# Later w_down load, finer warming products and short filler writes at the head of a scan-and-GeGLU kernel

## The chip, the core and the metric

The kernel runs on one core of one Trainium2 chip. The core has five engines with an instruction stream each: TensorE (PE: products, with its weight loads listed apart as PEld), VectorE (DVE), ScalarE (ACT), GpSimd (POOL) and SyncE (SP), which here does nothing but issue DMAs. They meet through semaphores. 16 DMA engines move data between the chip's memory (HBM) and the core's (SBUF), and PSUM holds the products. The metric is device microseconds of one execution. Before the change three runs took 179.32, 179.7 and 179.8 us, median 179.7.

## What is computed

The input x has 2048 tokens of 512 features. It is normalized, and goes through two branches that are multiplied at the end:

```python
xn = _layernorm(x, axis=-1)
s = _A_ref(xn, ...)                       # h = Lam_bar * h + Bu[t]; y = 2 Re(h C^T) + xn * Dskip
g = _silu((_gelu(xn @ w_gate) * (xn @ w_up)) @ w_down)
return x + s * g
```

The first branch is a complex diagonal recurrence over the tokens with 512 states; its parameters are dt = exp(log_dt), Lam_bar = exp(dt Lambda), and B scaled by (Lam_bar - 1) / Lambda. The second is a gated feed-forward with 1376 inner features. Types are bf16 with float32 sums.

## The kernel before

The tokens are worked in four slabs of 512, each of four tiles of 128 rows (m = 0 to 3). Nothing in the program loops: about 680 steps, each one a few instructions of one engine, are collected by `Plan.add`, and `Plan.run` emits them in the order of the fixed list `ORDER` (L21). The framework puts in the semaphore waits, from what each instruction reads and writes; the costs and ranks handed to `Plan.add` have no effect on the emitted program any more. So each engine, and SyncE's DMA queue as well, works its steps in the sequence in which they stand in `ORDER`.

The head of the program works on slab 0. The rows of x come in by single tiles (`load_x`, L222) between the four parts of w_up (`load_w`, L213). While x is on its way, TensorE runs products of a constant with itself (`dummies`, L300, seven of 512 columns, then `fill`, L304). VectorE has some `memset`s to do (L225, L250 to L254) and then waits. ScalarE loads its table with one Silu of one column (`tiny`, L257). With x there, `center` subtracts the mean (L341 on ScalarE and L343 on VectorE take half the sum each, L347 subtracts), `head_t` transposes on TensorE (L314, L329) and copies out (L320, L322), and `up_rows` (L402) multiplies by w_up. L615 to L650 work out the parameters and the tables of the recurrence, mostly on VectorE and GpSimd, and `first_w` (L432) makes the remaining up and gate products of slab 0. `first_at` (L445, L447) multiplies gate by up: the gated rows, tile `at`.

The gated rows have to be turned before the product with w_down. `at_t` (L479) does that with a transposing DMA from `at` to `atT`, tile by tile, and `down_pair` (L495) multiplies each tile's 11 blocks by w_down (`wd`), 11 products of 512 columns for a tile. Between the up and gate products of slab 0 and its down products stands `half` (L561), 32 products with the turned B for the recurrence. The scans run on VectorE (L573, L581, L592), and `y_tile` (L511 to L527) brings both branches together.

In the stretch that the change touches, SyncE issues in this order: the turn of xn (L378, two DMAs), B's two turns (L240), w_down's 1280 KB (L695), the turns of the gated rows of tiles 0, 2 and 1 (L479), the turn of slab 1's xn (L378), slab 2 of x (L217), the turn of tile 3's gated rows, and C's two turns (L743). TensorE's order there is the 32 products of L561, then L495 for tiles 0, 2 and 1, then more of L561.

In the listing, `early` is the list of VectorE steps that are to be done before x, and `sb` and `small` allocate SBUF tiles.

Of the kernel before, what the change touches and what calls it, by code (L numbers as in the profile page):

```python
# [10 lines left out]
AF = mybir.ActivationFunctionType  # L11
# [6 lines left out]
PE, ACT, DVE, POOL, SP = "PE", "ACT", "DVE", "POOL", "SP"  # L18


ORDER = (  # L21
# [23 lines left out]
)  # L45


# [33 lines left out]
def kernel(  # L81
# [18 lines left out]
    P = 128  # L100
# [20 lines left out]
    V, A, G, T = nc.vector, nc.scalar, nc.gpsimd, nc.tensor  # L121
    act = A.activation
# [5 lines left out]
    def sb(name, shape, dt=BF16):  # L128
        return consts.tile(shape, dt, name=name)
# [40 lines left out]
    ring = [psum.tile([P, D], FP32, name=f"ring{i}") for i in range(NR)]  # L170
    ybank = [psum.tile([P, D], FP32, name=f"ybank{i}") for i in range(2)]

    def small(name, w=NPT):
        return sb(name, [P, w], FP32)

    pl = Plan()
    DV, AC = 0.075, 0.075

    def dve(n, emit, reads=(), writes=(), rate=1.0, base=DV, **kw):
        return pl.add(DVE, base + n / 960.0 / rate, emit, reads, writes, lag=0.13, **kw)  # L180

    def acts(n, emit, reads=(), writes=(), ptr=0, **kw):
        return pl.add(ACT, AC + 0.12 * ptr + n / 1200.0, emit, reads, writes, lag=0.16, **kw)
# [55 lines left out]
    for ri, src in enumerate((A_B_re, A_B_im)):  # L239
# [9 lines left out]
    warm = nc.const_aps.tensor(1.0, [P, TS], BF16)  # L249
    early = [dve(1, lambda: V.memset(halfpi[:], math.pi / 2), writes=["halfpi"], rank=900.0),  # L250
             dve(4, lambda: V.memset(mhalf[:], -0.5), writes=["mhalf"], rank=900.0),
             dve(4, lambda: V.memset(e_t[:], math.e), writes=["e_t"], rank=900.0)]
    for i in range(NAT):
        early.append(dve(32, lambda i=i: V.memset(at[i][:, F:FP], 0.0), writes=[("atpad", i)], rank=900.0))  # L254
    one = nc.const_aps.tensor(1.0, [P, 1], FP32)

    acts(1, lambda: act(out=tiny[:], in_=one, func=AF.Silu), [], ["tiny"], rank=910.0, not_before=0.72)  # L257
    iota_i = sb("iota_i", [P, NBA], I32)
    iota_f = small("iota_f", NBA)

# [35 lines left out]

    def dummies(k, i):
        def f():
            for j in range(k):
                T.matmul(ybank[j][:] if j < 2 else ring[i][:], lhsT=warm[:, 0:P], rhs=warm, start=True, stop=True)  # L300
        pl.add(PE, k * 0.427, f, [], [("bank", i), ("y", 0), ("y", 1)], lag=0.22, not_before=0.6)

    def fill(w, i):
# [440 lines left out]
    for pt in range(NPT):  # L744
# [3 lines left out]
            out=C2[:, 0, pt, :], in0=CT[:, 0, pt, :], scalar=cre[:, pt : pt + 1], in1=tF[:, 1, :], op0=ALU.mult, op1=ALU.subtract),  # L748
            ["coef", ("CT", 0), ("tF",)], [("C2", 0, pt)], base=0.13)
        dve(512, lambda pt=pt: V.scalar_tensor_tensor(  # L750
            out=C2[:, 1, pt, :], in0=CT[:, 1, pt, :], scalar=ncre[:, pt : pt + 1], in1=tF[:, 0, :], op0=ALU.mult, op1=ALU.subtract),
# [104 lines left out]
```

## Time and profile before

| | us |
|---|---|
| runs | 179.32, 179.7, 179.8 |
| the profiled execution: its time | 179.31 |
| its span, first to last instruction | 177.5 |
| TensorE busy | 172.5 |
| VectorE busy | 157.5 |
| ScalarE busy | 123.9 |
| GpSimd busy | 11.3 |
| first L495 product starts at | 31.95 |

The span begins with the first instruction of the program, and all start times count from there; the 1.8 us between span and time lie around the program. A row of the time line gives start, length, engine, line and operation, output<-inputs, shape and count; in brackets stands how long the engine had been idle and what released it. A row of the chain has start, length and what ran. A row of waits gives total, times and longest. A row by stretches gives, for each engine, busy time and instructions, then the granted clock, the DMA share and GB/s. Lengths of TensorE products include the drain through the array, so that products 0.216 us apart are listed as 0.38 long. "SPq" rows are DMA issues: the length is that of the issue, not of the transfer.

### The profile page before, as it was taken

Reading aid. Unit: us, or ns where it says so; the run is one execution under the profiler, and the core shown is the slowest. Engines: PE = TensorE matmul, PEld = TensorE weight load, DVE = VectorE, ACT = ScalarE, POOL = GpSimd, SP = SyncE. Lnnn points to the kernel's source line nnn. Section 1 sums busy time; section 2 is a strip of 40 time slices with the busy share of each in tenths; the row PEclk is TensorE's granted clock in tenths of the full one; section 3 lists DMA queues with packets and bytes.
Section 4 is the critical chain, followed back from the end, with each engine's and each line's share of the span. In section 5 each row is a group of like instructions: output and inputs, shape, how many; then the busy total and the mean of one; then the engine's idle time right before and its main releaser. Section 6 shows DMA issues by size and latency. Waiting matters only on the chain.

```text
span 177.5 us, 2427 instructions
## 1 busy us (share of the span) xinstructions
PE 172.5 (97%) x846; PEld 82.3 (46%) x846; DVE 157.5 (89%) x256; ACT 123.9 (70%) x238; POOL 11.3 (6%) x26
## 2 busy tenths in 40 slices
PE   8999999899999999999999999999999999999992
PEld 3455453344455544444445454444444455444451
DVE  3678999999699994999979999899999999999754
ACT  6689989839999999899578855373148618572240
POOL 2472030000200000000040000000000000000000
PEclk9999999999999999999999999999999999999999
DMA  5999999999000709414000064094000006626122
GB/s 164 286 344 229 177 264 227 214 265 212 0 0 0 197 3 185 99 61 80 0 0 6 24 135 101 30 192 85 0 0 0 0 30 144 83 52 140 37 62 77
DMA packets 48355, 18.66 MB, mean 105 GB/s; under 512 B 40312, under 2 KB 47832, under 8 KB 48344
## 3 DMA queue, kind: packets, MB, share of 16 engines
q1 hardware_dynamic: 48344, 18.52, 47.7%
q8 instruction: 6, 0.10, 0.2%
q14 instruction: 5, 0.04, 0.1%
HBM read 6.46 MB, written 2.10 MB: 48 GB/s over the span
## 4 chain that ended last, share of the span: by engine, by line
PE 84%; DVE 7%; DMA 5%; POOL 2%; issue 0%; DVEq 0%
PE ring L463 31%; PE ring L495 22%; PE ybank L511 15%; PE ring L561 12%; DMA atT<-at 5%; PE ring L402 2%; DVE st L281 2%; DVE Q L650 1%; PE ring L300 1%; DVE yg L516 1%; DVE tab L650 1%; POOL dt__137 L618 1%; PE ybank L300 1%; DVE junk L522 1%; POOL rho L622 1%; POOL rs L293 0%
## 5 line engine op out<-in xcount | busy, mean ns | idle before, releaser
L463 PEld LDWEIGHTS <-xnT 128*128 128x128 bf16 x288 | 28.2, 98 | 28.4
L495 PE MATMUL ring<-wd,atT 128*128 128x512 bf16 (+1 forms) x176 | 39.4, 379 | 1.1 <-DMA atT<-at 1.1
L463 PE MATMUL ring<-wg,xnT 128*128 128x512 bf16 (+1 forms) x144 | 31.6, 357 | 0.0
L463 PE MATMUL ring<-wu,xnT 128*128 128x512 bf16 (+1 forms) x144 | 31.3, 357 | 0.0
L561 PE MATMUL ring<-xnT,BT 128*128 128x512 bf16 x128 | 30.1, 379 | 0.0
L592 DVE TENSOR_TENSOR_SCAN Fs<-rho,ini,W 128x512 bf16<-128x512 f32 x24 | 29.7, 1272 | 0.1
L466 ACT ACTIVATE ub<-ring 128x512 bf16<-128x512 f32 (+1 forms) x36 | 19.2, 555 | 13.7 <-PE ring L463 13.5
L511 PE MATMUL ybank<-C,hst 128*128 128x512 bf16 x120 | 27.7, 379 | 0.0
L495 PEld LDWEIGHTS <-atT 128*128 128x128 bf16 (+1 forms) x176 | 17.1, 98 | 22.1 <-DMA atT<-at 1.5
L563 ACT ACTIVATE U<-ring 128x512 bf16<-128x512 f32 x32 | 18.1, 599 | 7.3 <-PE ring L561 7.3
L466 ACT ACTIVATE gt<-ring 128x512 bf16<-128x512 f32 (+1 forms) x36 | 19.5, 556 | 3.7 <-PE ring L463 3.5
L498 ACT ACTIVATE g<-ring 128x512 f32<-128x512 f32 x16 | 9.4, 594 | 15.5 <-PE ring L495 15.3
L511 PEld LDWEIGHTS <-hst 128*128 128x128 bf16 x136 | 13.3, 98 | 14.0
L561 PEld LDWEIGHTS <-BT 128*128 128x128 bf16 x128 | 12.5, 98 | 14.8
L573 DVE TENSOR_TENSOR Q<-U,tab 128x4096 bf16<-128x4096 bf16 x8 | 18.3, 2289 | 0.9 <-ACT tab L657 0.7
L573 DVE TENSOR_TENSOR Q<-Fs,tab 128x4096 bf16<-128x4096 bf16 x8 | 18.3, 2288 | 0.1
L516 DVE TENSOR_TENSOR yg<-ybank,g 128x512 bf16<-128x512 f32 x15 | 10.2, 685 | 5.8 <-PE ybank L511 5.7
L774 ACT ACTIVATE junk<-x_tok 128x512 bf16<-128x512 bf16 x16 | 10.0, 632 | 1.3 <-DMA x_tok<-in_A_x_dram 1.3
L507 ACT ACTIVATE ybank<-sk 128x512 f32<-128x512 bf16 x15 | 9.1, 604 | 1.7 <-DVE yg L516 1.6
L779 ACT ACTIVATE xna<-x_tok,nb,rs 128x512 bf16<-128x512 bf16 x12 | 9.5, 812 | 0.0
L592 DVE TENSOR_TENSOR_SCAN Fs<-rho,W 128x512 bf16<-128x512 f32 x8 | 9.3, 1211 | 0.1
L472 DVE TENSOR_TENSOR at<-gt,ub 128x1024 bf16<-128x1024 bf16 x12 | 8.2, 684 | 0.0
(149 smaller groups left out, 172.0 us busy)
## 6 DMA issues: line engine op xcount, KB each, us to landing
x_tok<-in_A_x_dram SPq DMA_DIRECT2D x3, 512.0 KB, 4.2
out_dram<-ot SPq DMA_DIRECT2D x12, 128.0 KB, 2.1
wd<-in_B_w_down_dram SPq DMA_DIRECT2D x1, 1280.0 KB, 7.9
wu<-in_B_w_up_dram SPq DMA_DIRECT2D x4, 256.0 KB, 3.5
wg<-in_B_w_gate_dram SPq DMA_DIRECT2D x1, 864.0 KB, 8.0
x_tok<-in_A_x_dram SPq DMA_DIRECT2D x4, 128.0 KB, 4.2
wg<-in_B_w_gate_dram SPq DMA_DIRECT2D x1, 512.0 KB, 5.9
wu<-in_B_w_up_dram SPq DMA_DIRECT2D x1, 352.0 KB, 5.0
```

What stands on the lines that cost most here:

```text
L463: T.matmul(ps[:, 0 : b - a], lhsT=xnT[:, s % 2, m, k, :], rhs=wt[:, k, a:b], start=(k == 0), stop=(k == KT - 1))
L466: acts(b - a, lambda: act(out=dst[:, a:b], in_=ps[:, 0 : b - a], func=AF.Copy if up else AF.Gelu_apprx_tanh), [("bank", r)], [key], table= ...
L495: T.matmul(ps[:], lhsT=atT[:fs, k, m * P : (m + 1) * P], rhs=wd[:fs, k, :], start=(k == 0), stop=(k == NFT - 1))
L498: acts(512, lambda b=b, ps=ps: act(out=g2[gi][:, b, :], in_=ps[:], func=AF.Silu), [("bank", r)], [("g2", gi, b)], table="silu", rank=3.0)
L511: T.matmul(ps, lhsT=hst[s % 2][:, j // NPT, j % NPT, m * P : (m + 1) * P], rhs=C2[:, j // NPT, j % NPT, c0:c1], start=(j == 0 and not seed ...
L516: dve(w, lambda: V.tensor_tensor(out=yg[e][:, c0:c1], in0=ps, in1=g2[gi][:, b, c0:c1], op=ALU.mult), [key, ("g2", gi, b)], [("yg", e, c0)])
L561: T.matmul(ps[:], lhsT=BT[:, ri, k, pt * P : (pt + 1) * P], rhs=xnT[:, s % 2, :, k, :], start=(k == 0), stop=(k == KT - 1))
L563: acts(512, lambda q=q, ri=ri, ps=ps: act(out=U[ui][:, ri, q, :], in_=ps[:], func=AF.Copy), [("bank", r)], [("U", ui, q, ri)])
L573: dve(4096, lambda: V.tensor_tensor(out=Qf, in0=src.unsqueeze(1).to_broadcast(WQ), in1=table, op=ALU.mult), reads, ["Q"], rate=2.0)
L592: pl.add(DVE, 1.12 if s == 0 else 1.185, lambda ri=ri, q=q, pt=pt, first=first: V.tensor_tensor_scan(out=Fs[:, ri, q, :], data0=rho[:, pt ...
L774: acts(512, lambda i=i, fn=fn, sc=sc, m=m: act(out=junk()[:], in_=x_tok[:, s * M + m, :], func=fn, scale=sc, accum_out=sx[:, s, i, m : m + ...
L779: acts(512, lambda m=m: act(out=xn[m], in_=x_tok[:, s * M + m, :], func=AF.Identity, scale=rs[:, s, m : m + 1], bias=nb[:, s, m : m + 1]), ...
```

## The change

Four things change, all of them in what is issued in the first 25 us.

1. w_down's load (its step is 121 in the old list and 123 in the new one) stands behind the turn of tile 0's gated rows, step 162 in the new numbering, and ahead of tile 2's. Before, it stood right behind B's turns (steps 15 and 16).
2. `dummies` issues 28 products of 128 columns where it issued 7 of 512. They write the first 128 columns of the same banks: the first two the y banks, all others one ring bank.
3. A new step `pads` writes one column of a new tile `pad` 30 times on VectorE, last of what VectorE does before x.
4. A new step makes three Silus of one column into a new tile `tail2` on ScalarE, behind `tiny`.

All other numbers of `ORDER` are the old ones, renumbered for the two new steps (21 is `pads`, 27 the Silus); nothing else is moved. In the diff, the list is cut to the lines with these steps.

```diff
 ORDER = (
-    25, 26, 1, 29, 27, 24, 22, 23, 21, 2, 3, 4, 5, 6, 38, 19, 20, 17, 18, 0, 30, 31, 32, 39, 7, 8, 9, 10, 11, 28, 33, 35, 34, 36, 37, 54, 55, 57, 58,
...
-    15, 164, 168, 183, 165, 169, 228, 233, 16, 121, 166, 170, 185, 187, 167, 189, 231, 171, 230, 229, 184, 186, 362, 190, 188, 172, 173, 174, 176,
-    175, 177, 178, 179, 180, 181, 182, 191, 160, 237, 238, 162, 241, 242, 161, 239, 232, 245, 247, 262, 279, 287, 284, 283, 280, 286, 248, 263, 240,
...
+    26, 27, 28, 1, 31, 29, 25, 23, 24, 22, 2, 3, 4, 5, 6, 40, 19, 20, 17, 18, 0, 21, 32, 33, 34, 41, 7, 8, 9, 10, 11, 30, 35, 37, 36, 38, 39, 56, 57,
...
+    160, 161, 147, 15, 166, 170, 185, 167, 171, 230, 235, 16, 168, 172, 187, 189, 169, 191, 233, 173, 232, 231, 186, 188, 364, 192, 190, 174, 175,
+    176, 178, 177, 179, 180, 181, 182, 183, 184, 193, 162, 123, 239, 240, 164, 243, 244, 163, 241, 234, 247, 249, 264, 281, 289, 286, 285, 282, 288,
...
@@ -250,11 +250,19 @@
              dve(4, lambda: V.memset(e_t[:], math.e), writes=["e_t"], rank=900.0)]
+    pad = small("pad", 1)
+
+    def pads():
+        for _ in range(30):
+            V.memset(pad[:], 0.0)
+    early.append(pl.add(DVE, 0.90, pads, [], ["pad"], rank=900.0, not_before=0.72))
     for i in range(NAT):
...
     acts(1, lambda: act(out=tiny[:], in_=one, func=AF.Silu), [], ["tiny"], rank=910.0, not_before=0.72)
+    tail2 = small("tail2", 1)
+    acts(1, lambda: [act(out=tail2[:], in_=one, func=AF.Silu) for _ in range(3)], [], ["tail2"], rank=880.0)
...
     def dummies(k, i):
         def f():
-            for j in range(k):
-                T.matmul(ybank[j][:] if j < 2 else ring[i][:], lhsT=warm[:, 0:P], rhs=warm, start=True, stop=True)
+            for j in range(4 * k):
+                T.matmul((ybank[j][:] if j < 2 else ring[i][:])[:, 0:P], lhsT=warm[:, 0:P], rhs=warm[:, 0:P], start=True, stop=True)
         pl.add(PE, k * 0.427, f, [], [("bank", i), ("y", 0), ("y", 1)], lag=0.22, not_before=0.6)
```

40 rows, old and new, of the table ORDER are left out of this document.

## The prediction

> **What bounds the kernel now.** I read the page first (busy shares and the chain that ended last), then the waits of TensorE, then the time line around its one wait, and from there the queue that it waited for.
>
> ```profile
> PE 172.5 (97%) x846; PEld 82.3 (46%) x846; DVE 157.5 (89%) x256; ACT 123.9 (70%) x238; POOL 11.3 (6%) x26
> PE 84%; DVE 7%; DMA 5%; POOL 2%; issue 0%; DVEq 0%
> PE ring L495 <- DMA atT<-at: 1.1, 1, 1.1
> PE ybank L300 <- PEq L840: 0.8, 1, 0.8
> 23.83 7.07 PE L561 MATMUL ring<-xnT,BT 128*128 128x512 bf16 x32
> 31.95 0.39 PE L495 MATMUL ring<-wd,atT 128*128 128x512 bf16 x1 [1.06 <-DMA atT<-at]
> ```
>
> TensorE is busy 97% of the span, 84% of the last chain is its products, and behind the start of the program it waits once. The 32 products of L561 start 0.216 us apart ((7.07 - 0.38) / 31), so the last slot ends at 23.83 + 32 x 0.216 = 30.74; L495 opens at 31.95. That hole of 1.2 us is all that a better order can win. It also cuts the other way: whatever delays TensorE before 30.74 costs nothing until it has used up the 1.2 us.
>
> What the hole waits for is the chain in its stretch and the SyncE queue:
>
> ```profile
> 20.62 0.60 DVE at L445
> 21.13 0.34 DVE L447 TENSOR_TENSOR at<-gt,at 128x352 bf16<-128x352 bf16 x1
> 22.66 9.24 DMA atT<-at
> 19.89 2.04 SPq L240 DMA_TRANSPOSE BT<-in_A_B_im_dram  x1
> 21.98 0.58 SPq L695 DMA_DIRECT2D wd<-in_B_w_down_dram  x1
> 22.66 5.57 SPq L479 DMA_TRANSPOSE atT<-at  x1
> BT<-in_A_B_im_dram SPq DMA_TRANSPOSE x1, 4.5
> wd<-in_B_w_down_dram SPq DMA_DIRECT2D x1, 1280.0 KB, 7.9
> atT<-at SPq DMA_TRANSPOSE x16, 3.7
> L479 SPq DMA_TRANSPOSE atT<-at x16: 1262/1396/5568, 22.7 to 159.8; - x16
> ```
>
> (Start and length; for the queue rows the last number is the median time to landing.) The first gated rows are ready at 21.13 + 0.34 = 21.47, their turn is issued at 22.66 behind w_down's 1280 KB, and it takes 9.24 us where the median is 3.7: landed at 31.9. w_down itself lands at 21.98 + 7.9 = 29.9, the B turn before it at 19.89 + 4.5 = 24.4, so w_down has the queue for 5.5 us. L495 needs both.
>
> **The change, part by part.** *w_down behind the first turn.* On SyncE the 0.58 us issue is moved past one turn's issue (1.4 us by the median; the 5.57 came from standing behind w_down). The first turn no longer waits for w_down, and lands about 3.7 us after its issue. w_down starts when that turn is through, 5.5 us of queue as before. With nothing else changed: issue at 22.0, rows landed at 25.7, but not before B is out (24.4) plus a turn; w_down at 25.7 + 5.5 = 31.2 instead of 29.9. So the hole's end goes from 31.95 (rows) to about 31.2 (w_down): -0.7 us. Bounds: w_down moving as soon as it is issued, 23.4 + 5.5 = 28.9, so that the hole closes fully (-1.2); or its whole 7.9 us behind the end of its own issue, 24.0 + 7.9 = 31.9 (no gain). I take the middle one, since it is how w_down stood to the turn ahead of it in this trace. Queued behind it on SyncE: the second turn lands 2.0 us behind w_down (31.9 against 29.9 for the turn that stands there now), and L495's second group needs it 11 x 0.216 = 2.4 us after the first opens: covered by 0.4 us. The later items (third turn, next xnT, slab 2) have the same work ahead of them as before.
>
> *28 products of 128 columns for 7 of 512, and the head of the program.*
>
> ```profile
> 0.76 1.01 PE L300 MATMUL ybank<-const-bfloat16-1.0 128*128 128x512 bf16 x2 [0.76 <-PEq L840]
> 3.70 0.42 PE L304 MATMUL ring<-const-bfloat16-1.0 128*128 128x256 bf16 x1
> 3.80 0.47 PEld L314 LDWEIGHTS <-xna 128*128 128x128 bf16 x4 [0.38 <-DVE xna L347]
> 4.12 0.43 PE ring L314 x4
> 4.57 0.41 PE L329 MATMUL ybank<-ident,xna 128*128 128x128 bf16 x4
> 4.75 0.22 PE ybank L329 x4
> 4.98 3.04 PE ring L402 x14
> ```
>
> Four 128-column products with their weight loads take 0.43 us here (L314 in the chain), 0.107 each; 28 are 3.0 us against 3.70 - 0.76 = 2.94 now: +0.05. If the weight load sets the pace (0.47 / 4) it is 3.3 us, +0.35. Either way they end before x is ready on the rows below, so nothing lands on the path. By the same rows the array doubles its pace between L314 (0.107 each) and L329 (0.22 / 4 = 0.055), some 3.8 us after the first product.
>
> *30 one-column writes on VectorE.*
>
> ```profile
> 0.80 0.16 DVE L254 MEMSET at<- 128x16 uint32 x4 [0.80 <-PEq L840]
> L250 DVE MEMSET halfpi<- 128x1 f32 x1 | 0.1, 59 | 0.0
> 1.00 0.11 DVE L225 MEMSET pv<- 128x64 uint32 x1
> 2.79 0.49 DVE L343 TENSOR_SCALAR_CACHE_REDUCE yg<-x_tok 128x320 bf16<-128x320 bf16 x1 [1.67 <-DMA x_tok<-in_A_x_dram]
> 3.40 0.60 DVE L347 TENSOR_SCALAR xna<-x_tok,ma,mb 128x256 bf16<-128x256 bf16 x2
> 4.43 0.28 DVE L320 COPY W<-ring 128x256 bf16<-128x256 bf16 x1
> 45.91 0.16 DVE L788 SCALAR_TENSOR_TENSOR sx<-sx,mq 128x4 f32<-128x4 f32 x1
> 46.11 0.17 DVE L789 TENSOR_SCALAR sx<-sx 128x4 f32<-128x4 f32 x1
> ```
>
> VectorE idles 1.67 us before x. Writes to different tiles run 0.03 us apart (four in 0.16, each 0.07 long): 30 would take 0.9 us, hidden. But all 30 write the same tile. Where one VectorE instruction touches what the one before it wrote, the next starts 0.04 us after the first has ended (45.91 + 0.16 to 46.11). At 0.059 + 0.04, say 0.095 each, 30 take 2.85 us: from 1.04 to 3.9, and L343 starts 1.1 us later than 2.79. These are the two ends, 0 and 1.1 us. I take the long one: the writes share a tile, as L788 and L789 do and the four fast ones do not. Who waits: L347 (3.40 to 4.5), its transposes on TensorE (ready at 3.80, run from 3.91 behind the fill, so 1.0 late: 4.9), L320 behind them (about 0.9 late), and so the products of L402: d = 0.9 us on TensorE, with real gaps between 4.0 and 5.8.
>
> *Three more one-column Silus on ScalarE*, between the first one and x:
>
> ```profile
> 2.01 0.20 ACT L257 ACTIVATE tiny<-const-float32-1.0 128x1 f32<-128x1 f32 x1
> 2.79 0.36 ACT L341 ACTIVATE junk<-x_tok 128x192 bf16<-128x192 bf16 x1 [0.57 <-DMA x_tok<-in_A_x_dram]
> ```
>
> At 0.2 to 0.25 us each they end between 2.8 and 2.95; at worst 0.15 us late, under VectorE's 1.1. Without that cover: 0.15 us on the head.
>
> *Longer programs.* The change adds 42 instructions to TensorE, 30 to VectorE, 3 to ScalarE, and the program itself is fetched by the same DMA engines:
>
> ```profile
> q8 instruction: 1, 0.02, 16.1%
> 18.70:20.20 1.50, 1.50 (x10) 0.78 (x8) 1.47 (x4) 1.50 (x4) 0.00 (x0) 1.00 1.36 37
> 20.20:21.70 1.50, 1.50 (x9) 0.69 (x7) 1.50 (x4) 1.50 (x4) 0.00 (x0) 1.00 1.21 270
> ```
>
> A 16 KB block comes in between 17.9 and 18.4 (the first row is the DMA view of that stretch), and right behind it the B turn falls to 37 GB/s for 1.5 us, from about 270. TensorE passes 2 x 846 instructions in 177.5 us, 9.5 per us, so 42 more bring its block 4.4 us earlier, to about 14 us + d, amid plain loads. If the block is what stalls the turn, the B turns are out up to 1.3 us sooner. In the sum this is worth nothing, because the gated rows, not B, then start the first turn; it counts in a rival below. The bounds: -1.3 to +1.3 us on the queue (the stall may hit the xnT turns there).
>
> *The sum.* TensorE reaches L495 at 30.74 + 0.9 = 31.64. The gated rows, whose inputs come through TensorE and the parameter chain, are ready at 21.47 + 0.9 = 22.37, landed 26.07, w_down at 31.57. L495 opens at 31.65, 0.3 us earlier than now. Then the rest must follow:
>
> ```profile
> 47.83 0.75 DVE L750 SCALAR_TENSOR_TENSOR C<-hst,ncre,tF 128x512 bf16<-128x512 bf16 x1 [1.54 <-ACT tF L745]
> 64.23 0.69 DVE L581 TENSOR_TENSOR hst<-Q 128x1024 bf16<-128x1024 bf16 x1
> 65.51 0.59 PE L511 MATMUL ybank<-C,hst 128*128 128x512 bf16 x2
> ```
>
> VectorE, 0.9 us late, has a hole of 1.54 us before 47.83; the first L511 has 0.6 us between its last input (64.92) and its start. Both cover the shift, so the 0.3 us is kept to the end: 179.31 - 0.3 = 179.0 for the profiled execution, which is 0.4 under the median of the runs (179.7). Against the median: **179.4**.
>
> **The rivals.**
>
> *B, the writes are cheap* (0.03 us each, d = 0). Rows ready at 21.47, TensorE at 30.74. If the block is what stalls B, B is out at 23.1, the first turn lands at 21.5 + 3.7 = 25.2, w_down at 30.7: the hole is gone, -1.2, 178.5. For: the fast memsets, and the TensorE products that rewrite one bank without waiting. Against: L788/L789. The Trainium skill ("Runtime: NRT & Kernel Launch", Instruction fetch mechanics) calls the cost of crossing a 16 KiB block mostly hidden; by that B would still be out at 24.4 and w_down land at 31.2, -0.7 and 179.0. The 37 GB/s row speaks against the page.
>
> *C, slower: the array stays at half pace.* Now the products run without a gap from 0.76 to the doubling at about 4.57. With x 1.1 us late they stop at about 4.0. If the stretch must be unbroken and starts again at 4.9, full pace comes at 4.9 + 3.8 = 8.7, and the products from 5.8 to 8.7 run at half pace: 1.45 us lost, d = 2.35, beyond the hole by 1.15 us: 180.8. It decides once d exceeds 1.2. For: the doubling behind 3.8 dense us. Against: the gap starts when most of that stretch is over. The Trainium skill ("TensorE: Matmul & The Clock Gate", The HAM clock gate) has the pace released after one busy window of about 3.4 us that runs freely; by that, 4.0 - 0.76 = 3.2 us is just short, and the loss would be as worked out here. The trace agrees with the length, and shows no interrupted case.
>
> *D, slower: w_down takes the place of the rows.* Its 7.9 us behind its issue at 23.8 give 31.7 to 32.3, and a fetched block (1.3 us) in w_down or in the second turn puts L495 or its second group 0.9 us late: 180.6. For: nothing is faster in total on that queue, two transfers have only changed places. Against: 0.4 us of cover. Without the block it is no change, 179.7.
>
> **How the numbers follow.** A measurement of this kernel tells about 0.3% (0.54 us) from no change. Chances: my forecast 0.40 (178.9 to 179.9 by the bounds of its terms), B 0.22, C 0.20, D 0.18. Faster: a quarter of mine and most of B, 0.30. Slower: C, most of D and a tenth of mine, 0.39. The same: 0.31. The range reaches from B (178.5) to C (180.8).
>
> **What would show it.** In the new trace: the spacing of the 30 writes (0.03 or 0.095) and the start of L343 (2.8 or 3.9); the pace of L402 (0.216 or 0.43); the first turn's landing within about 4 us of its issue; L495's wait, now put down to w_down or gone; the stretch behind 18 us at 270 GB/s and the block's fetch near 15. The prediction is wrong if L343 starts on time, if L402 runs at half pace, or if a new wait of TensorE stands later in the chain.

## The result and the profile after

The changed kernel takes 181.41 us (median of 22 runs, 179.82 to 182.46) against 179.72 us before (22 runs): ratio 1.0085, 95% interval 1.0063 to 1.0106. It is slower by 1.7 us, where 179.4 us and a range of 178.5 to 180.8 us were predicted. The ratios, here and below, leave out a kernel's slow runs (three of ten at most), while the medians take in all of its runs. The profiled execution took 181.15 us with a span of 179.3 us, 1.84 us and 1.8 us more than before.

Lines of the page after, with the chain that ended last, and below it the waits of TensorE (total, times, longest):

```profile
PE 172.9 (96%) x851; PEld 84.8 (47%) x867; DVE 158.9 (89%) x286; ACT 124.3 (69%) x241; POOL 11.2 (6%) x26
...
PE 94%; DVE 3%; issue 2%; DVEq 0%
...
wd<-in_B_w_down_dram SPq DMA_DIRECT2D x1, 1280.0 KB, 7.6
```

```profile
PE ring L322 <- DVE xna L355: 1.6, 1, 1.6
```

The 1.1 us wait at the first down product is gone, as intended. DMA has left the chain altogether (5% before). In its place stands a new wait of 1.6 us, for the centred x, at the head of the program. The head and the early stages in the time line after (start, length, engine, line; everything behind the new writes stands 8 lines lower: L351 is the old L343, L410 the old L402, L569 the old L561, L503 the old L495, L455 the old L447, L487 the old L479, L703 the old L695):

```profile
1.07 3.58 DVE L257 MEMSET pad<- 128x1 f32 x29
4.69 0.48 DVE L351 TENSOR_SCALAR_CACHE_REDUCE yg<-x_tok 128x320 bf16<-128x320 bf16 x1
...
24.11 0.33 DVE L455 TENSOR_TENSOR at<-gt,at 128x352 bf16<-128x352 bf16 x1
...
3.70 0.42 PE L312 MATMUL ring<-const-bfloat16-1.0 128*128 128x256 bf16 x1
5.71 0.65 PE L322 MATMUL ring<-ident,xna 128*128 128x128 bf16 x4 [1.59 <-DVE xna L355]
...
6.79 2.48 PE L410 MATMUL ring<-wu,W 128*128 128x512 bf16 x6
...
10.83 0.39 PE L337 MATMUL ring<-ident,xna 128*128 128x128 bf16 x4
...
26.81 7.07 PE L569 MATMUL ring<-xnT,BT 128*128 128x512 bf16 x32
33.71 2.54 PE L503 MATMUL ring<-wd,atT 128*128 128x512 bf16 x10
...
19.27 2.15 SPq L240 DMA_TRANSPOSE BT<-in_A_B_re_dram  x1
...
24.47 1.38 SPq L487 DMA_TRANSPOSE atT<-at  x1
25.90 0.78 SPq L703 DMA_DIRECT2D wd<-in_B_w_down_dram  x1
```

Three things are to be read here. The first 29 of the 30 writes take 3.58 us, so one starts (3.58 - 0.06) / 28 = 0.126 us after another, and VectorE takes up x at 4.69 instead of 2.79: 1.90 us late. TensorE stands still from the end of its filler to 5.71. And then the first six of the up products (L410; the view ends at 9 us, and so does this row) run (2.48 - 0.38) / 5 = 0.42 us apart, half the array's pace; from the first of them to the transposes behind the fourteenth it takes 10.83 - 6.79 = 4.04 us, where 14 products at full pace are 3.03 us. The trace's record of the granted clock says the same: it begins, with full clock, at 8.84 us, where the kernel before has full clock from 4.62 us.

The delay adds up along TensorE. x's first transpose starts at 5.71 instead of 3.91 (1.80), the transposes themselves take 1.08 us instead of 0.90 (0.18), and the up products lose 4.04 - 3.03 = 1.01. That is 2.99 us, and the 32 products of L569 are through at 26.81 + 6.91 = 33.72 instead of 30.74: 2.98. The old hole of 1.21 us absorbs its share, and the first down product starts at 33.71 instead of 31.95, 1.76 us later. The span is 1.8 us longer, so nothing behind that point takes from or adds to the difference.

The first turn works as foreseen: issued at 24.47, when its rows are there (24.11 + 0.33), and no longer behind w_down. w_down lands at 25.90 + 7.6 = 33.5, just ahead of TensorE.

### The profile page after: what moved, and what is told of

Its sections match the earlier page's. It is cut to its first block, busy times and chain, and to the rows that moved or that the text cites. A ratio compares the mean times of both kernels' runs of the same rounds, so it can differ in the third digit from the quotient of the medians.

```text
span 179.3 us, 2485 instructions
## 1 busy us (share of the span) xinstructions
PE 172.9 (96%) x851; PEld 84.8 (47%) x867; DVE 158.9 (89%) x286; ACT 124.3 (69%) x241; POOL 11.2 (6%) x26
## 4 chain that ended last, share of the span: by engine, by line
PE 94%; DVE 3%; issue 2%; DVEq 0%
PE ring L471 31%; PE ring L503 21%; PE ring L569 15%; PE ybank L519 14%; PE ring L440 5%; PE ring L410 4%; PE ybank L440 2%; DVE pad L257 1%; DVE yg L524 1%; DVE junk L530 1%; PE ring L322 0%; PE ybank L337 0%; DVE xna L355 0%; PE ring L337 0%; PE ring L312 0%
## 5 line engine op out<-in xcount | busy, mean ns | idle before, releaser
L503 PE MATMUL ring<-wd,atT 128*128 128x512 bf16 (+1 forms) x170 | 38.9, 379 | 0.3
L569 PE MATMUL ring<-xnT,BT 128*128 128x512 bf16 x128 | 30.1, 379 | 0.0
L503 PEld LDWEIGHTS <-atT 128*128 128x128 bf16 (+1 forms) x176 | 17.1, 98 | 20.9 <-DMA atT<-at 0.3
L569 PEld LDWEIGHTS <-BT 128*128 128x128 bf16 x128 | 12.5, 98 | 14.7
L581 DVE TENSOR_TENSOR Q<-U,tab 128x4096 bf16<-128x4096 bf16 x8 | 18.3, 2289 | 0.9 <-ACT tab L665 0.7
L581 DVE TENSOR_TENSOR Q<-Fs,tab 128x4096 bf16<-128x4096 bf16 x8 | 18.3, 2287 | 0.1
(151 smaller groups left out, 177.9 us busy)
```

Of the source, the lines that this page charges most:

```text
L503: T.matmul(ps[:], lhsT=atT[:fs, k, m * P : (m + 1) * P], rhs=wd[:fs, k, :], start=(k == 0), stop=(k == NFT - 1))
L569: T.matmul(ps[:], lhsT=BT[:, ri, k, pt * P : (pt + 1) * P], rhs=xnT[:, s % 2, :, k, :], start=(k == 0), stop=(k == KT - 1))
L581: dve(4096, lambda: V.tensor_tensor(out=Qf, in0=src.unsqueeze(1).to_broadcast(WQ), in1=table, op=ALU.mult), reads, ["Q"], rate=2.0)
```

## The experiments

All of them are small edits of the changed kernel or of the kernel before. The table holds what decides: when VectorE takes up x, when TensorE is through with the 32 products (start of their row + 32 x 0.216), when w_down has landed (its issue plus its time to landing, by the trace), when the first down product starts, and the span. The ratio is to runs of the kernel before on the same chip.

| kernel | x | 32 products | w_down | first down product | span | median | ratio [95%] |
|---|---|---|---|---|---|---|---|
| before | 2.79 | 30.74 | 29.9 | 31.95 | 177.5 | 179.7 | 1 |
| changed | 4.69 | 33.72 | 33.5 | 33.71 | 179.3 | 181.41 | 1.0085 [1.0063, 1.0106] |
| without the writes | 2.77 | 31.20 | 30.3 | 31.19 | 176.8 | 179.04 | 0.9966 [0.9941, 0.9992] |
| a tile for each write | 2.78 | 30.99 | 31.4 | 31.40 | 177.4 | 179.16 | 0.9942 [0.9909, 0.9975] |
| moved load alone | 2.77 | 31.23 | 32.0 | 32.07 | 177.9 | 179.23 | 0.9954 [0.9928, 0.9981] |
| writes alone | 4.69 | 33.71 | 32.2 | 34.25 | 179.8 | 181.99 | 1.0114 [1.0089, 1.0139] |
| 52 warming products | 4.69 | 32.39 | 31.6 | 32.38 | 177.9 | 180.0 | 1.0025 [0.9996, 1.0055] |
| 14 writes | 2.87 | 31.28 | 30.3 | 31.27 | 176.8 | 179.1 | 0.9960 [0.9933, 0.9987] |
| 28 products alone | 2.77 | 31.01 | 30.2 | 32.29 | 177.8 | 179.67 | 0.9998 [0.9970, 1.0027] |
| load and products | 2.75 | 30.94 | 30.2 | 30.93 | 176.5 | 179.15 | 0.9965 [0.9937, 0.9993] |
| 22 writes | 3.70 | 31.66 | 32.0 | 32.09 | 177.8 | 180.02 | 1.0014 [0.9987, 1.0042] |
| 38 warming products | 4.70 | 32.40 | 32.7 | 32.70 | 178.9 | 179.98 | 1.0014 [0.9993, 1.0035] |
| coarse products, late x | 4.70 | 33.66 | 34.3 | 34.30 | 180.0 | 181.99 | 1.0089 [1.0044, 1.0134] |

In every row the span is the start of the first down product plus 145.5 to 146.2 us. To within 0.7 us, the changes of this case are decided by that one moment.

**Without the writes.**

```diff
     def pads():
-        for _ in range(30):
-            V.memset(pad[:], 0.0)
+        pass
```

> The changed kernel without its 30 one-column writes; the moved load, the 28 products and the three Silus stay. Theory (the writes are the loss: x 1.9 us late on VectorE, and about 1 us more while the array goes on at half pace): L343's counterpart starts near 2.8 again, the up products run 0.216 us apart from the first, the 32 products before the first down product end near 30.75, and what is left of the hole is w_down, landing between 30.4 and 31.2. Time 178.2 to 179.0, 0.4 to 0.8% under the kernel before. Rival (the moved load or the shifted program costs the time, the writes only hide it): w_down lands at 32 or later and the time stays at 180 or above.

Its time line (lines stand one higher than in the changed kernel: L350 is its L351), and the loading of w_down on its page:

```profile
2.77 0.49 DVE L350 TENSOR_SCALAR_CACHE_REDUCE yg<-x_tok 128x320 bf16<-128x320 bf16 x1 [1.65 <-DMA x_tok<-in_A_x_dram]
...
4.72 3.30 PE L409 MATMUL ring<-wu,W 128*128 128x512 bf16 x14
...
31.19 5.14 PE L502 MATMUL ring<-wd,atT 128*128 128x512 bf16 x23
...
23.84 0.60 SPq L702 DMA_DIRECT2D wd<-in_B_w_down_dram  x1
```

```profile
wd<-in_B_w_down_dram SPq DMA_DIRECT2D x1, 1280.0 KB, 6.5
```

179.04 us, ratio 0.9966, just above what was expected (at most 179.0): without the writes the rest of the change is a gain. x is on time, the up products run at full pace, w_down is there at 30.3, and TensorE goes into the down products without waiting. The rival, that the moved load itself costs the time, has fallen.

**A tile for each write.**

```diff
-    pad = small("pad", 1)
+    pad = [small(f"pad{i}", 1) for i in range(30)]
...
-        for _ in range(30):
-            V.memset(pad[:], 0.0)
+        for i in range(30):
+            V.memset(pad[i][:], 0.0)
```

> The changed kernel, but each of the 30 one-column writes goes to a tile of its own: as many instructions, no two on the same tile. Theory (a write that waits for the one before it costs 0.125 us, one that does not 0.03 us): the writes take about 0.9 us and end near 2.0, x is taken up at 2.8 as before, and the time is that of the kernel without the writes, 178.2 to 179.0. Rival (any 30 writes cost 0.125 us each): 181.2 to 181.6 as in the changed kernel. Second rival (the longer program moves its own loading into the way): writes short and x on time, but time at 180 or above.

```profile
1.07 0.83 DVE L257 MEMSET pad<- 128x1 f32 x30
2.78 0.48 DVE L351 TENSOR_SCALAR_CACHE_REDUCE yg<-x_tok 128x320 bf16<-128x320 bf16 x1 [0.88 <-DMA x_tok<-in_A_x_dram]
```

The same 30 instructions now take 0.83 us instead of 3.7: one starts (0.83 - 0.06) / 29 = 0.027 us after another. VectorE is done 0.88 us before x arrives, and the time is 179.16 us. Neither the number of writes nor the longer program costs anything; the order among writes to one tile, which the framework keeps with a wait, costs 0.1 us each.

**The moved load alone** (the kernel before, with one number moved):

```diff
-    15, 164, 168, 183, 165, 169, 228, 233, 16, 121, 166, 170, 185, 187, 167, 189, 231, 171, 230, 229, 184, 186, 362, 190, 188, 172, 173, 174, 176,
-    175, 177, 178, 179, 180, 181, 182, 191, 160, 237, 238, 162, 241, 242, 161, 239, 232, 245, 247, 262, 279, 287, 284, 283, 280, 286, 248, 263, 240,
+    15, 164, 168, 183, 165, 169, 228, 233, 16, 166, 170, 185, 187, 167, 189, 231, 171, 230, 229, 184, 186, 362, 190, 188, 172, 173, 174, 176,
+    175, 177, 178, 179, 180, 181, 182, 191, 160, 121, 237, 238, 162, 241, 242, 161, 239, 232, 245, 247, 262, 279, 287, 284, 283, 280, 286, 248, 263, 240,
```

> The kernel before with the moved load alone. Theory as in the prediction: the first turn lands about 4 us after its issue, w_down at 31.2 (bounds 30.0 and 31.9), L495 opens 0.7 us earlier: 179.0. Rival: w_down lands no earlier than the rows did (31.9 or later), 179.7 to 180.6.

```profile
4.98 3.53 PE L402 MATMUL ring<-wu,W 128*128 128x512 bf16 x14
...
32.07 4.27 PE L495 MATMUL ring<-wd,atT 128*128 128x512 bf16 x19 [0.68 <-DMA wd<-in_B_w_down_dram]
...
16.99 4.21 SPq L240 DMA_TRANSPOSE BT<-in_A_B_re_dram  x1
...
23.38 1.55 SPq L479 DMA_TRANSPOSE atT<-at  x1
```

179.23 us, ratio 0.9954: faster by 0.5%, as forecast. The one profiled execution (179.71 us) doesn't show it: w_down lands at 32.0, where the rival had it, and the first down product starts at 32.07. Two things came late in it. The pace doubled only among the up products (14 of them take 3.53 us, 3.19 at full pace); that moment differs between profiles (last section). And the issue of the first B turn took 4.21 us; that goes with the seven coarse products (the longer program, below). What the load's move gives is seen better where both are on time (load and products, below).

**The writes alone** (the kernel before, with the 30 writes):

```diff
+    pad = small("pad", 1)
+
+    def pads():
+        for _ in range(30):
+            V.memset(pad[:], 0.0)
+    early.append(pl.add(DVE, 0.90, pads, [], ["pad"], rank=900.0, not_before=0.72))
```

> The kernel before with the 30 writes alone (w_down in its old place, seven products of 512 columns, one Silu). Theory: TensorE comes to the first down product near 33.9 as in the changed kernel, and the rows' turn, behind w_down and with its rows 3 us later, lands near 34: 181.6 to 182.2. Rival (the finer products are what leaves the array at half pace): only the 1.9 us of x arrive there, less the 1.2 us of the hole: 180.4 to 180.8.

```profile
6.79 2.47 PE L410 MATMUL ring<-wu,W 128*128 128x512 bf16 x6
...
26.80 7.07 PE L569 MATMUL ring<-xnT,BT 128*128 128x512 bf16 x32
34.25 2.12 PE L503 MATMUL ring<-wd,atT 128*128 128x512 bf16 x9 [0.38 <-DMA atT<-at]
...
25.89 8.97 SPq L487 DMA_TRANSPOSE atT<-at  x3
```

181.99 us, ratio 1.0114. TensorE is through at 33.71, as in the changed kernel, at half pace in the same place, without the finer products. The rows' turn, behind w_down, lands at 34.2 and leaves a hole of its own. The writes alone account for the whole loss.

**52 warming products**, which bridge the gap.

```diff
-            for j in range(4 * k):
+            for j in range(4 * k + 24):
```

> The changed kernel with 24 more warming products (52 instead of 28), so that TensorE works on until x, late by the 30 writes, is there at 5.7. Theory (the 1.6 us gap sends the array back to the start of its warming, which costs about 1 us of half pace behind it): pace doubles near 4.5 and stays, the up products start at 0.216 us, TensorE comes to the first down product near 32.8 instead of 33.9, w_down lands about 1 us earlier as well, time 180.2 to 180.7. Rival (the pace does not depend on the gap, or w_down at 33.5 is the bound by itself): 181.2 to 181.6 as in the changed kernel.

```profile
0.93 4.82 PE L308 MATMUL ring<-const-bfloat16-1.0 128*128 128x128 bf16 x50
...
5.71 0.54 PE L322 MATMUL ring<-ident,xna 128*128 128x128 bf16 x4
...
6.46 2.77 PE L410 MATMUL ring<-wu,W 128*128 128x512 bf16 x11
...
32.38 3.84 PE L503 MATMUL ring<-wd,atT 128*128 128x512 bf16 x16
```

180.0 us, ratio 1.0025 [0.9996, 1.0055], clear of the changed kernel's 1.0085 [1.0063, 1.0106]. That is 0.2 us below what was expected. x is as late as there, its first transpose starts at the same 5.71, and nothing else was edited. But the array works until then and goes over to its full pace on the way (at 4.74; 50 products take 4.82 us, and 0.107 us each would be 5.3), and TensorE reaches the first down product at 32.38 instead of 33.71. So the gap costs 1.33 us (0.33 in the transposes, which take 0.75 instead of 1.08 us, and 1.0 in the up products, 3.04 us from the first to the transposes behind the fourteenth instead of 4.04), besides what the late x costs by itself.

**14 writes.**

```diff
-        for _ in range(30):
+        for _ in range(14):
```

> The changed kernel with 14 writes to the one tile instead of 30. Theory (they cost 0.125 us each, and only what reaches past x's arrival at 2.8 counts): they end at 1.07 + 14 x 0.125 = 2.82, x is taken up at 2.8 to 2.85, the rest is as without writes: 179.0 to 179.3. Rival (each write costs something wherever it stands): about half way, 180.2.

```profile
1.07 1.70 DVE L257 MEMSET pad<- 128x1 f32 x14
2.87 0.49 DVE L351 TENSOR_SCALAR_CACHE_REDUCE yg<-x_tok 128x320 bf16<-128x320 bf16 x1
```

179.1 us, ratio 0.9960. (1.70 - 0.06) / 13 = 0.126 us each again; they fit before x, and cost nothing.

**28 products alone** (the kernel before, with the new `dummies`).

```diff
-            for j in range(k):
-                T.matmul(ybank[j][:] if j < 2 else ring[i][:], lhsT=warm[:, 0:P], rhs=warm, start=True, stop=True)
+            for j in range(4 * k):
+                T.matmul((ybank[j][:] if j < 2 else ring[i][:])[:, 0:P], lhsT=warm[:, 0:P], rhs=warm[:, 0:P], start=True, stop=True)
```

> The kernel before with the 28 products of 128 columns for the seven of 512, nothing else. Theory as in the prediction (they end at the same time, and the block of program that comes in 4 us earlier is worth nothing in the sum, because w_down still stands ahead of the first turn): first turn landed at 31.7 to 32.0, 179.5 to 180.0. Rival (the earlier block clears the queue in front of B's turns, 1 us or more for everything behind): first turn landed at 30.8 or earlier, 178.8 to 179.2.

```profile
17.16 2.21 SPq L240 DMA_TRANSPOSE BT<-in_A_B_re_dram  x1
...
22.53 10.05 SPq L486 DMA_TRANSPOSE atT<-at  x3
...
32.29 4.06 PE L502 MATMUL ring<-wd,atT 128*128 128x512 bf16 x17 [1.11 <-DMA atT<-at]
```

179.67 us, ratio 0.9998. The issue of the first B turn isn't held up here (2.21 us), but that of the second takes 2.40, so that both are over at 21.81, as good as before (21.94), and the rows' turn, behind w_down, lands at 32.2. The prediction gave this term nothing, and within the 0.3% of the interval that is what it is worth.

**Load and products** (the changed kernel without the writes and without the three Silus).

```diff
     def pads():
-        for _ in range(30):
-            V.memset(pad[:], 0.0)
+        pass
...
-    acts(1, lambda: [act(out=tail2[:], in_=one, func=AF.Silu) for _ in range(3)], [], ["tail2"], rank=880.0)
+    acts(1, lambda: [], [], ["tail2"], rank=880.0)
```

> The kernel before with the moved load and the 28 products, without the writes and the three Silus. Theory: as without the writes alone, 178.8 to 179.2, w_down landing near 30.4, before or just when TensorE gets there; the Silus are worth nothing. Rival (the Silus cost or bring 0.1 to 0.2 us by way of ScalarE's half of the sum): 0.15 us away from that, which shows in the start of the first VectorE copy, not in the time.

```profile
3.63 0.27 PE L311 MATMUL ring<-const-bfloat16-1.0 128*128 128x256 bf16 x1
...
30.93 5.35 PE L502 MATMUL ring<-wd,atT 128*128 128x512 bf16 x23
...
21.06 0.34 DVE L454 TENSOR_TENSOR at<-gt,at 128x352 bf16<-128x352 bf16 x1
...
17.18 2.27 SPq L240 DMA_TRANSPOSE BT<-in_A_B_re_dram  x1
19.49 2.05 SPq L240 DMA_TRANSPOSE BT<-in_A_B_im_dram  x1
21.64 1.50 SPq L486 DMA_TRANSPOSE atT<-at  x1
23.18 0.91 SPq L702 DMA_DIRECT2D wd<-in_B_w_down_dram  x1
```

179.15 us, ratio 0.9965 [0.9937, 0.9993]. The Silus are worth nothing that these runs show (179.04 with them). w_down lands at 30.2, and the hole is closed: the first down product at 30.93, 1.02 us earlier than before. Against the products alone the move brings 0.5 us by the medians. This kernel, like the other four with x on time and the load moved, is faster than both the kernel before and the changed one.

**22 writes.**

```diff
-        for _ in range(30):
+        for _ in range(22):
```

> The changed kernel with 22 writes to the one tile instead of 30: x is taken up at 1.07 + 22 x 0.125 = 3.8, 1.0 us late as the prediction had it, and TensorE's gap before x's transposes is 0.6 to 0.7 us instead of 1.6. Theory A (any gap before the pace has doubled starts its stretch again): full pace comes 3 us after x's first transpose, near 7.7, about 1 us is lost, TensorE comes to the first down product near 32.7, and the time is 180.1 to 180.6. Theory B, the prediction's own case (the stretch goes on across a gap so short): full pace before 5.8, first down product at 31.6 to 31.8, time 179.0 to 179.5.

```profile
4.71 0.65 PE L322 MATMUL ring<-ident,xna 128*128 128x128 bf16 x4 [0.59 <-DVE xna L355]
...
5.75 3.19 PE L410 MATMUL ring<-wu,W 128*128 128x512 bf16 x14
...
32.09 6.21 PE L503 MATMUL ring<-wd,atT 128*128 128x512 bf16 x28 [0.26 <-DMA wd<-in_B_w_down_dram]
...
19.95 2.90 SPq L240 DMA_TRANSPOSE BT<-in_A_B_im_dram  x1
22.95 1.60 SPq L487 DMA_TRANSPOSE atT<-at  x1
```

This is close to the prediction's own case: x is taken up 0.9 us late, where the prediction had 1.1. Theory B has the pace right: with a gap of 0.59 us all 14 up products run 0.216 us apart, and TensorE is through at 31.66 (31.64 was predicted; that the two agree so closely is luck, since x is 0.2 us less late and the transposes, in part at half pace, take 1.04 us instead of 0.90). The time is between the two expectations, 180.02 us, because w_down came at 32.0 and not at 31.57.

**38 warming products** (30 writes).

```diff
-            for j in range(4 * k):
+            for j in range(4 * k + 10):
```

> The changed kernel with 10 more warming products (38): they run past the doubling, as the 24 more did, but stop near 4.8, so that a gap of about 0.9 us stands between the doubling and x's transposes at 5.7. Theory A (a gap costs only when it falls into the stretch before the doubling; a pace once granted outlives 0.9 us): the up products start 0.216 us apart, time as with 24 more, 179.8 to 180.4. Theory B (any gap takes the pace back): the up products start 0.43 us apart until 8.5 or later, time 181.1 to 181.6.

```profile
4.76 0.42 PE L312 MATMUL ring<-const-bfloat16-1.0 128*128 128x256 bf16 x1
5.70 0.55 PE L322 MATMUL ring<-ident,xna 128*128 128x128 bf16 x4 [0.52 <-DVE xna L355]
...
6.49 2.76 PE L410 MATMUL ring<-wu,W 128*128 128x512 bf16 x12
```

179.98 us, ratio 1.0014: Theory A's time, but the run doesn't test what it was made for. The filler at 4.76 is still at half pace (0.42 us long; 0.27 at full pace), so the doubling came behind the gap, not ahead of it. It is a second case of a gap of half a microsecond that didn't hold the doubling back. No run here puts a gap of 0.9 us behind the doubling.

**The changed kernel with the load in its old place.**

```diff
-    176, 178, 177, 179, 180, 181, 182, 183, 184, 193, 162, 123, 239, 240, 164, 243, 244, 163, 241, 234, 247, 249, 264, 281, 289, 286, 285, 282, 288,
+    176, 178, 177, 179, 180, 181, 182, 183, 184, 193, 162, 239, 240, 164, 243, 244, 163, 241, 234, 247, 249, 264, 281, 289, 286, 285, 282, 288,
```

(and 123 behind 16 in the line above it.)

> The changed kernel with w_down's load in its old place; the 30 writes, the 28 products and the Silus stay. The move: by the comparison with and without it when x is on time (0.3 to 0.5%), the time is 0.3 to 0.5% above the changed kernel, 181.9 to 182.3; rival, with TensorE at 33.7 the move has nothing left to win, 181.4. The pace: this run has the same 1.6 us gap. If the stretch starts again with the product behind the gap, the pace doubles at 8.8 once more; if the chip watches fixed stretches of time that do not follow the kernel, the doubling falls elsewhere, before the gap or between 7 and 9.1.

181.64 us, ratio 1.0059 [1.0020, 1.0098]. The interval holds the changed kernel's 1.0085 and, nearly, the 1.0114 of the writes alone. Inconclusive: whether the move is worth anything when x is late is not shown.

```profile
6.79 4.41 PE L410 MATMUL ring<-wu,W 128*128 128x512 bf16 x14
```

Its one profiled execution took 183.18 us, 1.5 us above the median, and is no measure of the move. But it has the gap of 1.6 us too, and full clock only from 9.25 us on, 3.5 us behind x's first transpose: neither at 8.8 nor in the stretch that was named for the other case.

**The changed kernel with the seven coarse products.**

```diff
-            for j in range(4 * k):
-                T.matmul((ybank[j][:] if j < 2 else ring[i][:])[:, 0:P], lhsT=warm[:, 0:P], rhs=warm[:, 0:P], start=True, stop=True)
+            for j in range(k):
+                T.matmul(ybank[j][:] if j < 2 else ring[i][:], lhsT=warm[:, 0:P], rhs=warm, start=True, stop=True)
```

> The changed kernel with the seven products of 512 columns instead of the 28 of 128; the moved load, the 30 writes and the Silus stay. The 28 products are worth nothing: 181.2 to 181.6, as the changed kernel; rival, the finer products set the array back, 180.4 or less. The pace: the same gap of 1.6 us once more; doubling at 8.8 again speaks for a stretch that starts with the product behind the gap, any other moment for fixed stretches of time.

```profile
6.79 4.15 PE L410 MATMUL ring<-wu,W 128*128 128x512 bf16 x14
```

181.99 us, ratio 1.0089, that of the changed kernel (the median is 0.4 us above what was expected): within the half percent of its interval, the finer products neither help nor hurt. The 14 up products take 4.15 us, 0.96 more than the 3.19 at full pace. The clock record has full clock from 8.74 us on here, and from 8.84 in the changed kernel and 8.83 with the writes alone, each time with a gap of 1.6 us and 3.0 to 3.1 us behind x's first transpose.

The single runs say that this loss isn't paid every time. Of the 48 executions of the four kernels with the 1.6 us gap (the changed one, the writes alone, and these last two), eight have spans of 177.9 to 178.7 us, like those of the kernel whose gap is bridged (177.9 to 179.4), and all others 178.9 or more. None of the eight was profiled.

## Why the prediction was wrong

**The failed term: the price of the 30 writes.** The prediction saw that the writes share a tile and must wait for one another, and took the long end of its two bounds: 0.059 + 0.04 us, "say 0.095 each", x 1.1 us late. They cost 0.126 us each, and x was 1.90 us late. The gap of 0.04 us was read between two instructions of 0.16 us; behind one of 0.06 us it is 0.066. Only the bound was wrong, not the reason: with a tile for each write, the same 30 writes cost 0.027 us each and nothing on the path. The Trainium skill ("VectorE: DVE Perf Modes", The DRAIN you can't avoid) reports of eight copies that a semaphore behind each costs nothing extra, and says that a next instruction that isn't held starts earlier. The traces agree with the second: without the wait the writes overlap (0.027 us apart, each 0.06 long), with it they don't. So for writes this small, other than for the eight copies, the wait has a price.

**The failed step: the array's pace.** The forecast had d = 0.9 us on TensorE and no loss of pace in its sum; half pace was its rival C, with a chance of 0.20, and C's outcome is what came. The first down product started at 33.71, where 31.65 was forecast. Of these 2.06 us, 0.75 are the price of the writes (at full pace x's lateness brings TensorE 1.65 us late, as the 52 warming products show, instead of 0.9), and 1.33 the lost pace. C had worked the loss out as 1.45 us, near the 1.33; its 180.8 us is too low because it goes with x 1.1 us late. Its reason, a stretch that must be unbroken and starts again behind the gap, is not what the traces show: a gap of 0.59 us (22 writes) did not put the doubling off, and the last section has what decides. The 52 warming products show that it is the gap and not the late x: with x as late, 1.33 us come back. With a gap of 0.59 us the forecast's way of counting d was sound; its own gap of 0.9 us was not tried.

**w_down.** The move does what it says: moved load alone 0.9954, load and products with the hole closed at 30.93. But for its own case the prediction had w_down at 31.57, and with 22 writes it came at 32.0. The sentence that fails there is that "the gated rows, not B, then start the first turn". (In the changed kernel it holds, since x is later still: B's second turn was issued by 23.88, the rows were ready at 24.44, and the turn went out at 24.47.) With 22 writes the rows were ready on time, at 22.39 (22.37 predicted), but the issue of the second B turn ended at 19.95 + 2.90 = 22.85, and the turn was issued at 22.95. With load and products it is the same: rows at 21.40, B's issue over at 21.54, turn at 21.64. SyncE's own issues, not the rows, start the first turn there. That is 0.5 us, and by the 22 writes it would have made the predicted 179.4 us 180.0 us (ratio 1.0014, interval 0.9987 to 1.0042: the half microsecond is read from the trace, and the times alone don't show it). The term behind it, 5.5 us from the first turn's landing to w_down's, came out at 4.1 to 5.5 us in the kernels with the moved load.

**The longer program.** The first turn of B in the kernel before, and with the writes alone:

```profile
16.51 3.34 SPq L240 DMA_TRANSPOSE BT<-in_A_B_re_dram  x1
```

```profile
19.27 3.37 SPq L240 DMA_TRANSPOSE BT<-in_A_B_re_dram  x1
```

TensorE's block was expected at 14 us + d, 14.9 by the forecast's d. In the ten profiles with 28 or more of the finer products it comes in at 14.4 to 15.4, whether x is late or not, and the issue of the first B turn takes 1.65 to 2.27 us. In the four with the seven coarse ones (before, moved load alone, writes alone, coarse products) it comes in at 18.3 to 21.3, each time during that issue, which takes 3.2 to 4.2 us. So the prediction's "if the block is what stalls the turn" is borne out. Between the moved load alone and load and products the first turn starts 1.7 us earlier in the profile (21.64 against 23.38). In the times it isn't shown: 0.9965 with the products against 0.9954 without. That it is worth nothing by itself (0.9998) was right.

**What was right.** The 28 products end when the seven did (the filler starts at 3.70 in both). The Silus don't matter. The first turn lands 3.6 us after its issue, and the wait for the rows is gone. Nothing behind the first down product takes a part of the shift: the slack at 47.83 and at the first L511 covers it, as the constant 145.5 us show.

## What to carry to other kernels

Filler on a waiting engine is free only if it ends before the wait does, and its length is set by the waits inside it: give each small write its own tile, or the framework chains them at 0.126 us instead of 0.027. A late input at the head costs twice, once by itself (x 1.9 us late brings TensorE 1.65 us late at full pace) and once more when TensorE runs out of warming products before its pace has doubled (1.33 us in the profiles here, though by the spans not in every execution), so let the warming products last until the latest time at which the data may come. Where the tail of a kernel has no slack and no waits, find the moment from which the rest is constant (here the first down product, 145.5 us before the end) and judge each edit by it.

## What the runs showed of the hardware

The moment at which the array's pace doubles is tied neither to the kernel's start nor to TensorE's first product, which stands at 0.76 in all profiles. The trace records when full clock is granted and when it is taken back behind the last products: at 8.84 and 179.51 us in the changed kernel, at 4.62 and 178.70 in the kernel before. (For the time ahead of the first entry the views print a clock of 1.00, though the products there run at half pace.) In all 14 profiles the two moments are a whole number of 3.413 us apart: 50 of them in the four with the gap of 1.6 us, 51 in the others. This is what a clock gives that is decided once every 3.413 us, at moments that follow a beat of their own. Without a gap full clock came between 3.5 us (load and products) and 5.7 us (moved load alone), with gaps of half a microsecond at 5.7 and 6.0, and with the gap of 1.6 us at 8.7, 8.8, 8.8 and 9.3.

By these profiles, what is decided on is how much of the last 3.413 us TensorE has worked. Full clock came behind ten such stretches with 81% of work or more that held no gap of 1.6 us (81% with load and products, 83 and 85% with the gaps of half a microsecond). It did not come behind the four that the gap of 1.6 us left with 53 to 65%; in the changed kernel that is the stretch from 2.02 to 5.43 us, in which TensorE worked until 4.12. There it came one stretch later, and that is the loss. Where between 65 and 81% the line runs was not measured. Once granted, full clock is kept with less: near the end of the program with 22 writes it outlived a stretch with 47% of work. So in an execution whose moment falls ahead of the gap, the gap may well cost nothing; the eight short executions above would fit that, but no trace shows one. The Trainium skill ("TensorE: Matmul & The Clock Gate", The HAM clock gate) describes the clock as a window of about 3.4 us that runs freely and isn't reset by a kernel. The traces agree with that, at 3.413 us; the scatter of the doubling without a gap, 3.5 to 5.7 us, is wider than the half microsecond either way that the page gives.

A single profile of this kernel is a poor witness for half a percent. The moved load alone is faster by 0.46% over its runs, and its profiled execution shows a longer span (177.9 us) than that of the kernel before (177.5 us).
